# Last-window remainders as fp32 products in column groups, and side-by-side high and low tokens, in an attention + mixture-of-experts kernel

## The chip, the cores and the metric

One NeuronCore of a Trainium2 chip runs the whole kernel. The metric is device time in microseconds, the median of the runs. Names: PE is TensorE's matmul row, PEld its weight loads, DVE is VectorE, ACT is ScalarE, POOL is GpSimd, SP is SyncE, which issues the weight transfers.

## What is computed

Eight sequences of 576 tokens go through windowed attention (8 heads of 64, window 128, a distance bias), which gives 512 numbers per token, `x`. Each token then goes to one of eight experts:

```
e = argmax(logits[b, s])  if s == 0 or local_gate[b, s] < 0.5  else  the expert of token s-1
h = np.maximum(x[b, s] @ w1[e], 0.0)          # 512 -> 1024
out[b, s] = p[e] * (h @ w2[e])                # 1024 -> 512, p is the softmax gate
```

## The kernel before

The first third is attention, with an order of instructions written out by hand. It writes `x` to a DRAM table. After that the experts are run in **visits**: a list of (expert, number of rows) that is fixed when the program is built, in blocks of 32 rows. `PLAN` has three own visits (8, 12 and 12 blocks) and then twelve by rank: 16, 9, 12, 8, 12, 8, 12, 7, 14, 9, 6 and 5 blocks. Each is run by `Fixed.run`, one behind the other.

A visit with N = 32 x blocks rows has eight steps f (128 of the 1024 hidden units each). In step f, `h` (128 hidden x N rows, in PSUM) is the sum of four slices kc of three products each, and then `second(f-1)` adds the step before to the results `y`: one PSUM tile of 128 rows x 512 for each **window** of 128 rows, again three products per window and step. Three products stand for one, because each fp32 number is split into a high and a low float32r part (`cut` for weights, `xh`, `xl` in `qx` for tokens, `hh`, `hl` for hidden values): `three` (L1058) issues high x high, high x low and low x high at L1060, L1061 and L1062. `windows` (L51) gives the starts of the windows; the last one is moved back so that it is whole, and overlaps the one before it where the number of blocks is no multiple of 4 (9 blocks: starts 0, 4 and 5). Rows computed twice are dropped by the index table when results are scattered.

Between the two layers ACT makes `hh = relu(h)` (L1108) and DVE makes `hl = max(h, 0) - hh` (L1109). `second(f-1)` stands behind `h` of step f on PE, so this pair of instructions has the time of one `second` and one `h` to be done. At a visit's end `finish` scales each `y` by the gate, alternately on ACT (L1069) and DVE (L1067), and POOL scatters it (L1047).

Weights come in chunks of 512 KB, eight to a visit (`a` for the first layer, `b` for the second, alternating), 120 in all. `Stream.load` issues a transfer on SP's queue into one of six `wraw` buffers (L264); `Stream.split` makes the high part on ACT (L269, two casts per chunk) and the low part on DVE (L271, two subtractions), into one of six `cut` buffers. A chunk is split as soon as a `cut` buffer is free, so up to six are ready ahead. While visits run, `Feed` gathers the rows of later visits on POOL and turns them (`split_x`: DVE transpose L209, ACT cast L213, DVE subtraction L215). Engines take their instructions in program order, so each of these pieces also delays what stands behind it on its engine.

Of the kernel before, what the change touches and what calls it, by code (L numbers as in the profile page):

```python
# [10 lines left out]
F32 = mybir.dt.float32  # L11
F32R = mybir.dt.float32r
# [3 lines left out]
ALU = mybir.AluOpType  # L16
# [32 lines left out]


def windows(nb):  # L51
    return [min(4 * t, nb - 4) for t in range((nb + 3) // 4)]


PLAN = _plan()
# [45 lines left out]
def moe_attention(ctx, tc, qT, kT_d, vv, wg, wl, w1, w2, out):  # L101
# [32 lines left out]
    msel_last = cp.tile([P, 3, 4], F32, name="msel_last")  # L134
# [33 lines left out]
    def run(g):  # L168
        for _ in g:
            pass  # L170
# [103 lines left out]
    class Stream:  # L274


        def __init__(self, order):
            self.order = order
            self.raw, self.cut, self.gone, self.n_raw, self.n_cut, self.first, self.depth = [], {}, set(), 0, 0, 0, 1

        def load(self):
            while self.n_raw < len(self.order) and self.n_raw < self.n_cut + RAWS:
                e, which, c = self.order[self.n_raw]
                self.raw.append(load_chunk(e() if callable(e) else e, which, c))
                self.n_raw += 1

        def fill(self):
            while self.n_cut < len(self.order) and self.n_cut < self.first + self.depth:
                self.load()
                run(self.split(self.room(), now.act, nc.vector))  # L290
            self.load()

# [3 lines left out]

        def split(self, c, scalar, vector):
            raw = self.raw.pop(0)
            self.cut[self.n_cut] = c[:, 0], c[:, 1]
            self.n_cut += 1  # L300
            yield from split_chunk(raw, c, scalar, vector)
# [28 lines left out]
    FIXED_ORDER = [(w, c) for c in range(4) for w in "ab"]  # L330
    FLEX_ORDER = [(w, c) for w in "ab" for c in range(4)]
    order, by_rank = [], [expert_reg(r) for r in range(NE)]
    for kind, e, _, nb in PLAN:
        order += [(e if kind == "own" else by_rank[e], w, c) for w, c in (FLEX_ORDER if nb == 4 else FIXED_ORDER)]
    W = Stream(order)

    vp = ctx.enter_context(tc.tile_pool(name="vp", bufs=4))


    with ExitStack() as actx:  # L340
# [90 lines left out]
        def setup():  # L431

            whole = dict(channel_multiplier=0, allow_small_or_imprecise_dtypes=True)
            for a in (V[0][1][64:128], *zero_p(1), *zero_q(1), V[1][1][64:128], part[:, P + 64:]):
                pool.memset(a, 0.0)
                yield
            pool.memset(w32, 0.0)
            nc.sync.dma_start(w32[:, :, 0:8], wg.rearrange("(k p) e -> p k e", p=P))
            nc.sync.dma_start(w32[:, :, 8:9], wl.rearrange("(k p) e -> p k e", p=P))
            yield  # L440
            pool.memset(onesb, 1.0)
            yield
# [12 lines left out]
            pool.memset(first[0:1, 0:1], 1.0)  # L455
            yield
            pool.memset(msel_last, 0.0)
            yield
            for n in range(1, 4):
                pool.tensor_copy(msel_last[:, n - 1, 4 - n:], msel[:, 4 - n:])  # L460
# [322 lines left out]
        def indices(t, idx, x0, c0, visits):  # L783

            xi, rw, sc = idx
            wins = [(at + w, min(4, nb - 4 * i)) for at, nb in visits for i, w in enumerate(windows(nb))]
# [15 lines left out]
            while lo < n:  # L802
                hi = lo + 1
                at, new = wins[lo]
                while new == 4 and hi < n and wins[hi] == (wins[hi - 1][0] + 4, 4):
                    hi += 1
                sel = msel if new == 4 else msel_last[:, new - 1]
# [253 lines left out]
        nc.tensor.matmul(o, ah, bl, start=False, stop=False)  # L1061
        nc.tensor.matmul(o, al, bh, start=False, stop=stop)  # L1062

    def finish(o, g, col, alt):
        y = mp.tile([P, DM], F32, name="y", bufs=4)
        if alt:
            nc.vector.tensor_scalar(y, o, g, None, ALU.mult)  # L1067
        else:
            now.act.activation(y, o, AF.Copy, scale=g)  # L1069
        pending.append((col, y))  # L1070


    class Fixed:
        def __init__(self, rows):
            self.rows = rows

        def columns(self):
            return 96 * 32 * self.rows.blocks + 24 * DM * len(windows(self.rows.blocks))

        def run(self, W, tick):  # L1080
            N = 32 * self.rows.blocks
            wins = [slice(32 * w, 32 * w + P) for w in windows(self.rows.blocks)]
            n = len(wins)
            ys = [py.tile([P, DM], F32, name="y") for _ in range(n)]
            xh, xl = self.rows.xh[:, :, :N], self.rows.xl[:, :, :N]
            hs = {}

            def second(f):
                hh, hl = hs.pop(f)
                vh, vl = W.at("b")  # L1090
                for t, sl in enumerate(wins):
                    three(ys[t], hh[:, sl], hl[:, sl], vh[:, f % 2], vl[:, f % 2], f == 0, f == 7)
                    if t == n // 2 - 1:
                        tick()
                if f % 2:
                    W.done("b")

            for f in range(8):
                ah, al = W.at("a")
                hp = ph_.tile([P, N], F32, name="h")  # L1100
# [5 lines left out]
                hh = mp.tile([P, N], F32R, name="hh", bufs=3)  # L1106
                hl = mp.tile([P, N], F32R, name="hl", bufs=3)
                now.act.activation(hh, hp, AF.Relu)  # L1108
                nc.vector.scalar_tensor_tensor(hl, hp, 0.0, hh, ALU.max, ALU.subtract)  # L1109
                hs[f] = (hh, hl)  # L1110
                if f % 2:
                    W.done("a")
# [2 lines left out]
                    second(f - 1)  # L1115
                tick()
            second(7)
            for t in range(n):
                c = self.rows.t0 + t
                finish(ys[t], self.rows.g[:, t:t + 1], self.rows.idx[2][:, c:c + 1], t % 2)  # L1120


    class Flex:
# [238 lines left out]
```

## Time and profile before

| | us |
|---|---|
| median of 3 runs | 699.55 (698.94 to 699.76) |
| the profiled execution, its own time | 698.89 |
| its span in the profile | 697.2 |
| PE busy | 672.1 (96%) |
| DVE busy | 506.7 (73%) |
| ACT busy | 408.9 (59%) |
| POOL busy | 422.8 (61%) |

Busy time of PE is no measure of work done: products are pipelined, and each row's duration includes the time until its last results are out. The time that one product really costs is the step from its start to the start of the next.

### The profile page before, as it was taken

How to read it: one execution, taken by the hardware profiler on the slowest of the kernel's cores; microseconds unless marked ns; L12 is line 12 of the kernel's file. 1: busy time of each engine (PE TensorE's matmuls, PEld its weight loads, DVE VectorE, ACT ScalarE, POOL GpSimd, SP SyncE). 2: the span in 40 equal slices, each digit the busy share in tenths (PEclk: the TensorE clock that was granted, in tenths of full speed). 3: DMA queues.
4: the chain of work that ended last, by engine and by line, in shares of the span. 5: the costliest groups of instructions: out<-in, count | busy, mean ns of one | idle time of the engine just before them, and what ended most of it. 6: DMA issues, size and time to landing. Idle time of an engine off the chain costs nothing.

```text
span 697.2 us, 16242 instructions
## 1 busy us (share of the span) xinstructions
PE 672.1 (96%) x5377; PEld 563.1 (81%) x5377; DVE 506.7 (73%) x1738; ACT 408.9 (59%) x1157; POOL 422.8 (61%) x689
## 2 busy tenths in 40 slices
PE   8999999999889999999999999999999999999995
PEld 4777777777657778898888889899899888888994
DVE  7798988988887999996455985775675574455750
ACT  5987978979887753344334444554554563344540
POOL 8868678687896878077744554566467357151411
PEclk9999999999999999999999999999999999999998
DMA  8963753843643765364645555675675564355600
GB/s 269 316 210 121 236 178 122 263 152 115 198 153 101 234 228 181 117 200 156 176 139 170 166 173 152 216 228 165 195 224 176 187 212 161 122 177 162 210 31 20
DMA packets 65944, 122.23 MB, mean 175 GB/s; under 512 B 14177, under 2 KB 33249, under 8 KB 65858
## 3 DMA queue, kind: packets, MB, share of 16 engines
q1 hardware_dynamic: 56034, 101.27, 45.9%
q0 software_dynamic: 9392, 19.31, 9.2%
q8 instruction: 43, 0.70, 0.4%
q10 hardware_dynamic: 432, 0.59, 0.3%
q14 instruction: 43, 0.35, 0.1%
HBM read 102.14 MB, written 20.30 MB: 176 GB/s over the span
## 4 chain that ended last, share of the span: by engine, by line
PE 83%; DVE 6%; issue 4%; POOL 4%; ACT 2%; POOLq 0%; ACTq 0%; DVEq 0%
PE y L1062 10%; PE y L1060 10%; PE y L1061 10%; PE h L1061 10%; PE h L1062 10%; PE h L1060 10%; PE xa L188 7%; PE pt L188 6%; PE sc L188 6%; PE pk L188 3%; POOL ro_all L188 2%; DVE scs L188 1%; ACT cut L188 1%; POOL cut L188 1%; POOL out L1047 0%
## 5 line engine op out<-in xcount | busy, mean ns | idle before, releaser
L203 POOL DMA_INDIRECT kr<-xd,xidx x142 | 156.9, 1105 | 58.9 <-issue 42.7
L271 DVE TENSOR_TENSOR cut<-wraw,cut 128x512 fp32r<-128x512 f32 x232 | 151.1, 688 | 44.2 <-ACT cut L269 42.9
L269 ACT CAST cut<-wraw 128x512 fp32r<-128x512 f32 x218 | 124.3, 618 | 59.5 <-PE y L1062 57.8
L1061 PE MATMUL h<-qx,cut 128*128 128x384 f32 (+7 forms) x472 | 148.3, 314 | 0.2 <-DVE qx L215 0.2
L1062 PE MATMUL h<-qx,cut 128*128 128x384 f32 (+7 forms) x472 | 148.4, 314 | 0.0
L1060 PE MATMUL h<-qx,cut 128*128 128x384 f32 (+7 forms) x472 | 147.4, 313 | 0.0
L1047 POOL DMA_INDIRECT out<-y,sidx x41 | 44.7, 1089 | 145.2 <-ACT y L1069 117.6
L1062 PE MATMUL y<-cut,hl 128*128 128x512 f32 x328 | 129.6, 396 | 1.2 <-DVE hl L1109 1.1
L1060 PE MATMUL y<-cut,hh 128*128 128x512 f32 x328 | 130.0, 396 | 0.0
L1061 PE MATMUL y<-cut,hh 128*128 128x512 f32 x328 | 129.2, 394 | 0.0
L188 ACT ACTIVATE cut<-scs,mn 128x192 f32<-128x192 f32 (+1 forms) x288 | 124.8, 437 | 5.8 <-DVE mn L188 5.6
L188 POOL TENSOR_SCALAR cut<-cut,r 128x192 f32<-128x192 f32 (+1 forms) x288 | 116.1, 419 | 19.2 <-DVE r L188 9.9
L1108 ACT ACTIVATE hh<-h 128x384 fp32r<-128x384 f32 (+7 forms) x113 | 49.8, 441 | 124.1 <-PE h L1062 123.9
L1109 DVE SCALAR_TENSOR_TENSOR hl<-h,hh 128x384 fp32r<-128x384 f32 (+7 forms) x120 | 58.5, 488 | 77.0 <-ACT hh L1108 75.1
L1061 PEld LDWEIGHTS h<-qx,cut 128*128 128x128 f32 x472 | 89.2, 189 | 6.5 <-DVE qx L215 0.8
L1060 PEld LDWEIGHTS h<-qx,cut 128*128 128x128 f32 x472 | 89.3, 189 | 5.7
L1062 PEld LDWEIGHTS h<-qx,cut 128*128 128x128 f32 x472 | 89.2, 189 | 1.8
L188 PE MATMUL pt<-ident,cut 128*128 128x128 f32 x512 | 74.4, 282 | 2.4 <-POOL cut L188 2.3
L1062 PEld LDWEIGHTS y<-cut,hl 128*128 128x128 f32 x328 | 61.4, 188 | 16.6 <-DVE hl L1109 3.5
L188 DVE CUSTOM_DVE_ANT_0 scs<-sc,slopes 128x192 f32<-128x192 f32 (+1 forms) x224 | 67.4, 334 | 9.5 <-PE sc L188 6.3
L1060 PEld LDWEIGHTS y<-cut,hh 128*128 128x128 f32 x328 | 61.8, 188 | 9.7
L1061 PEld LDWEIGHTS y<-cut,hh 128*128 128x128 f32 x328 | 61.8, 188 | 9.6
(205 smaller groups left out, 976.8 us busy)
## 6 DMA issues: line engine op xcount, KB each, us to landing
wraw<-w SPq DMA_DIRECT2D x120, 512.0 KB
kr<-kT SPq DMA_DIRECT2D x31, 288.0 KB
qx<-qT SPq DMA_DIRECT2D x30, 288.0 KB
cut<-v SPq DMA_DIRECT2D x8, 1024.0 KB
xd<-T SPq DMA_DIRECT2D x8, 768.0 KB
xd<-T SPq DMA_DIRECT2D x8, 384.0 KB
kr<-xd,xidx POOLq DMA_INDIRECT x142, 3.9
qx<-qT SPq DMA_DIRECT2D x16, 64.0 KB
```

Of the source, the lines that this page charges most:

```text
L188: ins = getattr(self.engine, name)(*args, **kw)
L203: queued(nc.gpsimd.indirect_dma_start(out=r, out_offset=None, in_=src[0:n, :], in_offset=bass.IndirectOffsetOnAxis(ap=col, axis=0), bounds ...
L269: scalar.copy(c[:, 0, f], raw[:, f])
L271: vector.tensor_tensor(c[:, 1, f], raw[:, f], c[:, 0, f], ALU.subtract)
L1047: ins = nc.gpsimd.indirect_dma_start(out=out[:, :], out_offset=bass.IndirectOffsetOnAxis(ap=col, axis=0), in_=y, in_offset=None, bounds_ch ...
L1060: nc.tensor.matmul(o, ah, bh, start=start, stop=False)
L1061: nc.tensor.matmul(o, ah, bl, start=False, stop=False)
L1062: nc.tensor.matmul(o, al, bh, start=False, stop=stop)
L1108: now.act.activation(hh, hp, AF.Relu)
L1109: nc.vector.scalar_tensor_tensor(hl, hp, 0.0, hh, ALU.max, ALU.subtract)
```

## The change

1. `windows` no longer moves the last window back. Where the rest behind the whole windows is one or two blocks (32 or 64 rows; the visits of 9, 14, 9, 6 and 5 blocks), that rest has no float32r products any more. ACT takes relu of it into an fp32 tile `hr`, and `beside` multiplies `hr` with the raw fp32 weights `wraw`: four steps' products of 32 rows, or two steps' of 64 rows, stand in different column groups of TensorE and go to different partitions of one `y` tile. `finish` then adds the four (or two) partial sums on DVE, and takes this tile first. A rest of three blocks (the visit of 7) becomes a window of 96 rows.
2. The raw buffers of these visits' `b` chunks are kept until `beside` has read them.
3. In visits with fewer than 256 rows (7, 6 and 5 blocks) the first layer multiplies the high weights with high and low tokens side by side, in one product of 2N columns, and the low weights in one of N columns. ACT copies the half that belongs to the low tokens to SBUF (`ha`), DVE adds the other half, and DVE, not ACT, makes `hh`.

```diff
 def windows(nb):
-    return [min(4 * t, nb - 4) for t in range((nb + 3) // 4)]
+    return range(0, nb, 4)
...
         def load(self):
-            while self.n_raw < len(self.order) and self.n_raw < self.n_cut + RAWS:
+            while self.n_raw < len(self.order) and self.n_raw < min([self.n_cut, *self.kept]) + RAWS:
...
+            if self.n_cut in self.keep:
+                self.kept[self.n_cut] = raw
...
-    def finish(o, g, col, alt):
+    def finish(o, g, col, alt, groups=1):
         y = mp.tile([P, DM], F32, name="y", bufs=4)
+        m = o.shape[0] // groups
         if alt:
-            nc.vector.tensor_scalar(y, o, g, None, ALU.mult)
+            nc.vector.tensor_scalar(y[:m], o[:m], g[:m], None, ALU.mult)
         else:
-            now.act.activation(y, o, AF.Copy, scale=g)
-        pending.append((col, y))
+            now.act.activation(y[:m], o[:m], AF.Copy, scale=g[:m])
+        for j in range(1, groups):
+            nc.vector.scalar_tensor_tensor(y[:m], o[m * j:m * j + m], g[:m], y[:m], ALU.mult, ALU.add)
+        pending.append((col[:m], y[:m]))
...
+            def beside(f):
+                if f % 2:
+                    i = W.find("b")
+                    raws.append((i, W.kept[i]))
+                if f % groups < groups - 1:
+                    return
+                for j in range(groups):
+                    nc.tensor.matmul(ys[-1][m * j:m * j + m], rest[j], raws[j // 2][1][:, j % 2], start=f < groups, stop=f == 7,
+                                     skip_group_check=True)
...
             def second(f):
...
+                if m:
+                    beside(f)
+                for t in range(self.whole):
+                    sl = wins[t]
+                    three(ys[t][:sl.stop - sl.start], hh[:, sl], hl[:, sl], vh[:, f % 2], vl[:, f % 2], f == 0, f == 7)
...
-                    three(hp, ah[:, f % 2, cs], al[:, f % 2, cs], xh[:, kc], xl[:, kc], kc == 0, kc == 3)
+                    if both:
+                        passed[0] += 3 * N
+                        nc.tensor.matmul(hp.rearrange("p (two n) -> p two n", n=N), ah[:, f % 2, cs], self.rows.x[:, :, kc, :N],
+                                         start=kc == 0, stop=False, skip_group_check=True)
+                        nc.tensor.matmul(hp[:, :N], al[:, f % 2, cs], xh[:, kc], start=False, stop=kc == 3, skip_group_check=True)
+                    else:
+                        three(hp, ah[:, f % 2, cs], al[:, f % 2, cs], xh[:, kc], xl[:, kc], kc == 0, kc == 3)
...
-                now.act.activation(hh, hp, AF.Relu)
-                nc.vector.scalar_tensor_tensor(hl, hp, 0.0, hh, ALU.max, ALU.subtract)
+                if both:
+                    ha = mp.tile([P, N], F32, name="ha", bufs=2)
+                    now.act.copy(ha, hp[:, N:])
+                    nc.vector.tensor_tensor(ha, hp[:, :N], ha, ALU.add)
+                    hp = ha
+                w = P * self.whole if m else N
+                hh = mp.tile([P, N], F32R, name="hh", bufs=3)[:, :w]
+                hl = mp.tile([P, N], F32R, name="hl", bufs=3)[:, :w]
+                if m:
+                    rest.append(mp.tile([P, 64], F32, name="hr", bufs=8)[:, :m])
+                    now.act.activation(rest[-1], hp[:, w:], AF.Relu)
+                if both:
+                    nc.vector.tensor_scalar(hh, hp[:, :w], 0.0, None, ALU.max)
+                else:
+                    now.act.activation(hh, hp[:, :w], AF.Relu)
+                nc.vector.scalar_tensor_tensor(hl, hp[:, :w], 0.0, hh, ALU.max, ALU.subtract)
```

On PE, at the end of the last visit (5 blocks), before: `h` is a slice's first-layer product, `y` the second layer's; the six `y` products at the end are the last step's two windows.

```order
L1060 MATMUL h<-qx,cut 128x160
L1061 MATMUL h<-qx,cut 128x160
L1062 MATMUL h<-qx,cut 128x160
L1060 MATMUL y<-cut,hh 128x512
L1061 MATMUL y<-cut,hh 128x512
L1062 MATMUL y<-cut,hl 128x512
L1060 MATMUL y<-cut,hh 128x512
L1061 MATMUL y<-cut,hh 128x512
L1062 MATMUL y<-cut,hl 128x512
```

The same place after the change: two products per slice, and in front of the last step's only whole window the remainder's four fp32 products of steps 4 to 7.

```order
L1140 MATMUL h<-qx,cut 128x320
L1142 MATMUL h<-qx,cut 128x160
L1069 MATMUL y<-cut,hh 128x512
L1070 MATMUL y<-cut,hh 128x512
L1071 MATMUL y<-cut,hl 128x512
L1112 MATMUL y<-wraw,hr 32x512 x4
L1069 MATMUL y<-cut,hh 128x512
L1070 MATMUL y<-cut,hh 128x512
L1071 MATMUL y<-cut,hl 128x512
```

Six products of the second window are gone from each pair of steps, and the four side by side stand in front of the whole window's.

On DVE, from the end of the second visit of 9 blocks into the visit of 6, before:

```order
L1109 SCALAR_TENSOR_TENSOR hl<-h,hh 128x288
L271 TENSOR_TENSOR cut<-wraw,cut 128x512 x2
L1067 TENSOR_SCALAR y<-y,gs 128x512
L271 TENSOR_TENSOR cut<-wraw,cut 128x512 x2
L1109 SCALAR_TENSOR_TENSOR hl<-h,hh 128x192 x2
```

The same place after the change; `ha` is the sum of both halves of `h`:

```order
L1162 SCALAR_TENSOR_TENSOR hl<-h,hh 128x256
L271 TENSOR_TENSOR cut<-wraw,cut 128x512 x2
L1081 SCALAR_TENSOR_TENSOR y<-y,gs 32x512 x2
L271 TENSOR_TENSOR cut<-wraw,cut 128x512 x2
L1081 SCALAR_TENSOR_TENSOR y<-y,gs 32x512
L1150 TENSOR_TENSOR ha<-h,ha 128x192
L1159 TENSOR_SCALAR hh<-ha 128x128
L1162 SCALAR_TENSOR_TENSOR hl<-ha,hh 128x128
L1150 TENSOR_TENSOR ha<-h,ha 128x192
```

Three additions of partial sums take the place of one scaling, and each step of the short visit has three DVE instructions instead of one.

On ACT, in the visit of 6 blocks after the change:

```order
L1149 COPY ha<-h 128x192
L269 CAST cut<-wraw 128x512 x2
L1157 ACTIVATE hr<-ha 128x64
L1149 COPY ha<-h 128x192
L269 CAST cut<-wraw 128x512 x2
L1157 ACTIVATE hr<-ha 128x64
```

Before, one `hh<-h` stood in the place of the copy and of the relu; now the relu of the rest (`hr`, which PE's fp32 products read) waits for DVE's sum and stands behind two casts.

## Rows read from the trace of the kernel before

**Rows 1.** The page: busy time, and the slices of PE and its clock.
```profile
PE 672.1 (96%) x5377; PEld 563.1 (81%) x5377; DVE 506.7 (73%) x1738; ACT 408.9 (59%) x1157; POOL 422.8 (61%) x689
PE   8999999999889999999999999999999999999995
PEclk9999999999999999999999999999999999999998
```

**Rows 2.** Windows: the visits of 9, 7, 14, 9, 6, 5 blocks, in time.
```profile
core 0: us, PE busy (x) PEld busy (x) DVE busy (x) ACT busy (x) POOL busy (x), PEclk, DMA share, GB/s
374.60:406.00 31.40, 31.40 (x199) 27.16 (x198) 26.14 (x78) 13.87 (x28) 16.63 (x17) 1.00 0.56 177
552.30:574.70 22.40, 22.36 (x146) 19.69 (x145) 17.66 (x33) 14.21 (x30) 14.58 (x13) 1.00 0.68 223
574.70:616.10 41.40, 41.40 (x193) 36.03 (x192) 19.63 (x32) 15.90 (x30) 16.92 (x16) 1.00 0.47 147
616.10:645.40 29.30, 29.30 (x169) 26.17 (x168) 17.16 (x30) 13.91 (x28) 11.07 (x12) 1.00 0.56 170
645.40:667.20 21.80, 21.80 (x146) 19.78 (x146) 14.98 (x29) 12.94 (x28) 7.70 (x7) 1.00 0.55 174
667.20:689.20 22.00, 22.00 (x145) 19.51 (x143) 6.96 (x15) 6.53 (x16) 2.24 (x2) 1.00 0.04 16
```

**Rows 3.** Timeline of PE around 600 us: start, duration, instruction (14 blocks).
```profile
599.72 0.36 PE L1060 MATMUL h<-qx,cut 128*128 128x448 f32 x1
599.92 0.36 PE L1061 MATMUL h<-qx,cut 128*128 128x448 f32 x1
...
600.55 0.40 PE L1061 MATMUL y<-cut,hh 128*128 128x512 f32 x1
600.79 0.39 PE L1062 MATMUL y<-cut,hl 128*128 128x512 f32 x1
```

**Rows 4.** Timeline of PE: 7 blocks behind a `y` product; then 9 blocks.
```profile
570.33 0.40 PE L1062 MATMUL y<-cut,hl 128*128 128x512 f32 x1
570.56 0.26 PE L1060 MATMUL h<-qx,cut 128*128 128x224 f32 x1
570.66 0.28 PE L1061 MATMUL h<-qx,cut 128*128 128x224 f32 x1
570.77 0.27 PE L1062 MATMUL h<-qx,cut 128*128 128x224 f32 x1
...
639.83 0.29 PE L1061 MATMUL h<-qx,cut 128*128 128x288 f32 x1
639.96 0.29 PE L1062 MATMUL h<-qx,cut 128*128 128x288 f32 x1
```

**Rows 5.** Timeline of PE around 671 us, 5 blocks, behind a `y` product.
```profile
671.00 0.40 PE L1062 MATMUL y<-cut,hl 128*128 128x512 f32 x1
671.23 0.23 PE L1060 MATMUL h<-qx,cut 128*128 128x160 f32 x1
671.31 0.27 PE L1061 MATMUL h<-qx,cut 128*128 128x160 f32 x1
671.42 0.27 PE L1062 MATMUL h<-qx,cut 128*128 128x160 f32 x1
```

**Rows 6.** Timeline of PE around 123 us, fp32 products of attention.
```profile
122.58 1.19 PE L188 MATMUL pk<-xT,w 128*32 128x128 f32 x40
123.70 0.59 PE L188 MATMUL sc<-kr,qx 128*128 128x192 f32 x2
124.13 0.60 PE L188 MATMUL pt<-ident,cut 128*128 128x128 f32 x4
124.57 0.38 PE L188 MATMUL pk<-ident,part 128*128 128x128 f32 x2
```

**Rows 7.** Timeline of PE around 242 us: another tile form between float32r products.
```profile
242.16 0.28 PE L1062 MATMUL h<-qx,cut 128*128 128x256 f32 x1
242.28 0.28 PE L1060 MATMUL h<-qx,cut 128*128 128x256 f32 x1
242.49 0.38 PE L188 MATMUL pk<-identb,rcb 128*1 128x128 f16 x4
242.80 0.39 PE L1061 MATMUL h<-qx,cut 128*128 128x256 f32 x1
243.02 0.28 PE L1062 MATMUL h<-qx,cut 128*128 128x256 f32 x1
```

**Rows 8.** Groups of DVE by form: busy us, mean ns, idle before.
```profile
L271 DVE TENSOR_TENSOR cut<-wraw,cut 128x512 fp32r<-128x512 f32 x232 | 151.1, 688 | 44.2 <-ACT cut L269 42.9
L1109 DVE SCALAR_TENSOR_TENSOR hl<-h,hh 128x512 fp32r<-128x512 f32 x8 | 5.5, 691 | 13.0 <-ACT hh L1108 13.0
L1109 DVE SCALAR_TENSOR_TENSOR hl<-h,hh 128x192 fp32r<-128x192 f32 x8 | 2.8, 355 | 2.5 <-ACT hh L1108 2.5
L188 DVE TENSOR_TENSOR trk<-trk,tr 128x128 f32<-128x128 f32 x4 | 1.1, 271 | 0.0
L188 DVE TENSOR_SCALAR slopes<-qx 128x128 f32<-128x128 f32 x4 | 0.8, 249 | 0.3 <-POOL qx L188 0.3
```

**Rows 9.** Waits by engine and cause, 552 to 575 us.
```profile
DVE qx L215 <- ACT qx L213: 2.2, 4, 0.7
DVE cut L271 <- ACT cut L269: 2.0, 2, 1.2
```

**Rows 10.** Waits by engine and cause, 645 to 690 us: total, times, longest.
```profile
DVE qx L215 <- ACT qx L213: 1.1, 2, 0.7
```

**Rows 11.** The group of casts on ACT; below it SP's waits from 300 us on.
```profile
L269 ACT CAST cut<-wraw 128x512 fp32r<-128x512 f32 x218 | 124.3, 618 | 59.5 <-PE y L1062 57.8 <-DMA wraw<-w 1.5
SPq L264 <- DVE cut L271: 269.4, 82, 7.0
```

**Rows 12.** Timeline at the end of the last visit, all engines.
```profile
688.58 0.69 ACT L1069 ACTIVATE y<-y,gs 128x512 f32<-128x512 f32 x1 [1.83 <-PE y L1062]
...
688.84 0.40 PE L1062 MATMUL y<-cut,hl 128*128 128x512 f32 x1
689.28 0.75 DVE L1067 TENSOR_SCALAR y<-y,gs 128x512 f32<-128x512 f32 x1 [2.17 <-PE y L1062]
689.54 0.98 POOL L1047 DMA_INDIRECT out<-y,sidx  x1 [19.35 <-ACTq L1312]
690.83 0.99 POOL L1047 DMA_INDIRECT out<-y,sidx  x1 [0.30 <-issue]
```

More of the change, by code (lines that the diff above doesn't have):

```diff
@@ L133, in moe_attention @@
     quart = cp.tile([P, 4], F32, name="quart")
-    msel_last = cp.tile([P, 3, 4], F32, name="msel_last")
+    msel_part = cp.tile([P, 3, 4], F32, name="msel_part")
     roff = cp.tile([P, 1], F32, name="roff")
@@ L278, in __init__ @@
             self.order = order
+            self.keep, self.kept = set(), {}
             self.raw, self.cut, self.gone, self.n_raw, self.n_cut, self.first, self.depth = [], {}, set(), 0, 0, 0, 1
         def load(self):
-            while self.n_raw < len(self.order) and self.n_raw < self.n_cut + RAWS:
+            while self.n_raw < len(self.order) and self.n_raw < min([self.n_cut, *self.kept]) + RAWS:
                 e, which, c = self.order[self.n_raw]
@@ L289, in fill @@
                 self.load()
+                if not self.raw:
+                    break
                 run(self.split(self.room(), now.act, nc.vector))
@@ L332, in moe_attention @@
     order, by_rank = [], [expert_reg(r) for r in range(NE)]
+    kept = set()
     for kind, e, _, nb in PLAN:
+        if nb % 4 in (1, 2):
+            kept |= {len(order) + i for i, (w, _) in enumerate(FIXED_ORDER) if w == "b"}
         order += [(e if kind == "own" else by_rank[e], w, c) for w, c in (FLEX_ORDER if nb == 4 else FIXED_ORDER)]
     W = Stream(order)
+    W.keep = kept
     vp = ctx.enter_context(tc.tile_pool(name="vp", bufs=4))
@@ L456, in setup @@
             yield
-            pool.memset(msel_last, 0.0)
+            pool.memset(msel_part, 0.0)
             yield
             for n in range(1, 4):
-                pool.tensor_copy(msel_last[:, n - 1, 4 - n:], msel[:, 4 - n:])
+                pool.tensor_copy(msel_part[:, n - 1, :n], msel[:, :n])
                 yield
@@ L785, in indices @@
             xi, rw, sc = idx
-            wins = [(at + w, min(4, nb - 4 * i)) for at, nb in visits for i, w in enumerate(windows(nb))]
+            wins = [(at + w, min(4, nb - w)) for at, nb in visits for w in windows(nb)]
             m, n = t.shape[1], len(wins)
@@ L806, in indices @@
                     hi += 1
-                sel = msel if new == 4 else msel_last[:, new - 1]
+                sel = msel if new == 4 else msel_part[:, new - 1]
                 dve.tensor_tensor(fw[:, lo:hi], t[:, at:at + 4 * (hi - lo)].rearrange("p (c q) -> p c q", q=4),
@@ L1075, in __init__ @@
             self.rows = rows
+            self.n, part = rows.n, rows.last(rows.n - 1)
+            self.part = part if part < 3 else 0
+            self.whole = self.n - (self.part > 0)
         def columns(self):
-            return 96 * 32 * self.rows.blocks + 24 * DM * len(windows(self.rows.blocks))
+            return 96 * 32 * self.rows.blocks + (24 * self.whole + 8 * self.part) * DM
         def run(self, W, tick):
             N = 32 * self.rows.blocks
-            wins = [slice(32 * w, 32 * w + P) for w in windows(self.rows.blocks)]
-            n = len(wins)
-            ys = [py.tile([P, DM], F32, name="y") for _ in range(n)]
+            wins = [slice(P * t, min(P * t + P, N)) for t in range(self.n)]
+            ys = [py.tile([P, DM], F32, name="y") for _ in wins]
             xh, xl = self.rows.xh[:, :, :N], self.rows.xl[:, :, :N]
-            hs = {}
+            hs, rest, raws = {}, [], []
+            m = 32 * self.part
+            groups = P // m if m else 1
+            both = N < 256
+            def beside(f):
[7 more added lines that the diff above has]
+                                     skip_group_check=True)
+                passed[0] += 4 * DM
+                for i, _ in raws:
+                    del W.kept[i]
+                del rest[:groups]
+                raws.clear()
             def second(f):
@@ L1090, in second @@
                 vh, vl = W.at("b")
-                for t, sl in enumerate(wins):
-                    three(ys[t], hh[:, sl], hl[:, sl], vh[:, f % 2], vl[:, f % 2], f == 0, f == 7)
-                    if t == n // 2 - 1:
+                if m:
[3 more added lines that the diff above has]
+                    three(ys[t][:sl.stop - sl.start], hh[:, sl], hl[:, sl], vh[:, f % 2], vl[:, f % 2], f == 0, f == 7)
+                    if t == (self.n + 1) // 2 - 1:
                         tick()
@@ L1099, in run @@
                 ah, al = W.at("a")
[L1100 removed]
+                hp = ph_.tile([P, 2 * N if both else N], F32, name="h")
                 for kc in range(4):
                     cs = slice(P * kc, P * kc + P)
[L1103 removed]
+                    if both:
[5 more added lines that the diff above has]
+                        three(hp, ah[:, f % 2, cs], al[:, f % 2, cs], xh[:, kc], xl[:, kc], kc == 0, kc == 3)
                     if kc == 1:
                         tick()
[L1106 to L1109 removed]
+                if both:
[14 more added lines that the diff above has]
+                nc.vector.scalar_tensor_tensor(hl, hp[:, :w], 0.0, hh, ALU.max, ALU.subtract)
                 hs[f] = (hh, hl)
@@ L1117, in run @@
             second(7)
-            for t in range(n):
+            for i, t in enumerate([self.n - 1, *range(self.n - 1)] if m else range(self.n)):
                 c = self.rows.t0 + t
-                finish(ys[t], self.rows.g[:, t:t + 1], self.rows.idx[2][:, c:c + 1], t % 2)
+                rows = P if m and t == self.n - 1 else wins[t].stop - wins[t].start
+                finish(ys[t][:rows], self.rows.g[:, t:t + 1], self.rows.idx[2][:, c:c + 1], i % 2 and groups < 4, rows // (wins[t].stop - wins[t].start))
     class Flex:
```

## The prediction

> **What bounds the kernel now.** First the page: PE is busy for 96% of the span at the full clock, and DVE, the next, for 73% [rows 1]. That is an average, so I then cut out the visits that the change touches (the width of `h` in PE's timeline marks them). In each of the six PE is busy all the time, at a granted clock of 1.00 (2.4 GHz), while DVE's load differs: 17.66 of 22.40 us with 7 blocks, 14.98 of 21.80 with 6, 6.96 of 22.00 with 5 [rows 2]. So a product less on PE is time gained, but in the visits of 7 and 6 blocks DVE has only 5 and 7 us to spare.
>
> Third, what a product costs: the step from start to start. A `y` product of 512 columns takes 0.23 us, an `h` product of 448 columns 0.20 [rows 3], one of 288 columns 0.13 [rows 4]. Narrower ones gain nothing: with 224 and with 160 columns the step is 0.11, except just behind a `y` product, where it is 0.10 and 0.08 [rows 4, 5]. I read this as the weights' load showing: behind a long product the next weights are in place, behind a short one they are not.
>
> **The change, part by part.**
>
> *Removed.* Five visits (9, 14, 9, 6, 5 blocks) lose their last window: 8 steps of 3 products, 24 per visit, 120 in all. 120 x 0.23 = -27.6 us.
>
> *Added fp32 products.* No fp32 product of 512 columns is in the trace. The nearest are attention's: four fp32 instructions of 128 columns start at 124.13, the next group at 124.57, so 0.11 each [rows 6], about twice the float32r price per column. The tokens' logits are 20 products per sequence in the code (16 of 128 columns, 4 of 64) and 40 instructions in the row, so an fp32 product is two instructions. Those 40 stand in column groups of 32 (the row's 128*32). One behind another they would need 32 x 0.11 + 8 x 0.055 = 4.0 us; they took 1.12 (122.58 to 123.70) [rows 6]. So four groups do run side by side. At 512 columns an instruction is then 4 x 0.107 = 0.43 us, and a set of two or four products side by side 0.86. Rests of 32 rows (9, 9, 5 blocks) need two sets per visit, rests of 64 rows (14, 6) four: 6 + 8 = 14 sets, +12.0 us. One behind another, the 40 products would cost 34.4; that is the upper end, and 12.0 the lower.
>
> *Changing the form.* Each set stands between float32r products of the whole array. A small tile form between such products costs 0.09 on entry (242.28 to 242.49, where 0.12 is usual), about 0.08 on the way back (four products of 128 columns, 0.23, take 0.31) and 0.10 at the step after (0.22 instead of 0.12) [rows 7]: 0.27 per set, +3.8 us. With 512 columns behind it the last 0.10 may be hidden: lower end 2.4.
> The Trainium skill (TensorEngine Tiling (Array Packing), section Key Properties) says that changing the tiling mode drains TensorE. Taken at its word, each of 28 changes would wait out the tail of a product, 0.40 - 0.23 = 0.17 us [rows 3], which makes 4.8 us in place of 3.8, and the forecast 1 us later; the row's 0.09 and 0.08 say less than a whole drain. I keep 3.8.
>
> *Side by side.* 7, 6 and 5 blocks have 32 slices each, now three steps of 0.11 (0.33). After: one product of 448, 384 or 320 columns and one of 224, 192 or 160. The long ones cost 0.20, 0.174 and 0.145 (the latter two on the line from 0.13 at 288 to 0.20 at 448). Each short one stands behind a long one, as in the two places where the step was 0.10 and 0.08; for 192 columns I take 0.09. Gains per slice: 0.03, 0.07 and 0.11; times 32: 1.0, 2.2 and 3.6, -6.8 us. If the short product cost its 0.11 here too, it would be -4.7.
>
> PE's own work: -27.6 + 12.0 + 3.8 - 6.8 = **-18.6 us**.
>
> *DVE in the short visits.* Each step gets a sum (`ha`) and a max (`hh`), and with 6 and 5 blocks a narrower `hl`. Neither is in the trace. Nearest: a sum of an SBUF and a PSUM tile of 128 columns, 0.271; a tensor-scalar of 128 columns, 0.249; the slope over columns from `hl`, (0.691 - 0.355) / 320 = 1.05 ns [rows 8]. So per step 0.37 + 0.35 with 224 columns; 0.34 + 0.25 - 0.07 with 192; 0.31 + 0.25 - 0.03 with 160. Over eight steps: +5.8, +4.2 and +4.2.
>  - 7 blocks: 17.66 + 5.8 = 23.5 us of DVE against 22.4 - 1.0 = 21.4 of PE. It no longer fits: a stall of 2.1, if the 4.2 us in which DVE now waits for ACT's casts [rows 9] fill up.
>  - 6 blocks: 14.98 + 4.2 + three additions for the 9 blocks' rest at about 0.69 (an `hl` of 512 columns has that length [rows 8]) - 0.3 for the scaling they replace = 20.9; 1.1 in which DVE waits for ACT's token casts [rows 10] does not go away: 22.0. PE needs 21.8 - 5.5 + 4 x 1.13 - 2.2 = 18.6. Stall 3.4.
>  - 5 blocks: 11.2 of DVE in 15.1 of PE, but at the start the sum for step 0 stands behind a scaling and an addition of the visit before (0.75, 0.69) and two subtractions (1.3): ready after 3.3 us, while PE has two `h`, 8 x 0.22 = 1.8. Stall 1.5. And `hr` waits on ACT for DVE's sum, behind casts of 0.62 [rows 11]: 0.4 at each of two sets. Together 2.3.
>
> In all +7.8 us. Its lower end is 0 (chunks are split up to six ahead, which would have to absorb it), its upper end twice this, if ACT and DVE wait for each other at each step.
>
> *The end.* Now ACT scales the first `y` while PE still runs, DVE the second; scatters start at 689.54 and 690.83 [rows 12]. After, the rest's tile needs ACT (0.69) and three dependent additions (3 x 0.69) once its last set is done, 0.8 us before PE's end. So it is ready 2.0 us after PE instead of 0.3, and the other scatter queues behind it on POOL: +2.0.
> In other visits the additions are covered by two `h` of the visit that follows (3 us or more with 8 or more blocks).
>
> *Raw buffers kept longer.* Loads wait for a buffer now (269 us on SP's queue), and yet casts waited only 1.5 us in the whole run for a load [rows 11]. Priced 0, covered by the chunks split ahead; without that cover late loads of the last two visits could cost some 3 to 5 us. *A rest of 96 rows* (7 blocks): same number of products, 0. *Index tables*: a few small DVE instructions, 0.
>
> **Sum.** -18.6 + 7.8 + 2.0 = -8.8 us. The profiled execution took 698.89, 0.66 under the median, so 690.1 for it and **690.8 for the median**.
>
> **Rivals.**
>  - *DVE's additions are hidden.* For it: DVE has idle time in all three visits, and chunks are ready ahead. Against: program order puts subtractions between the new instructions. Then -18.6 + 2.0: 683.0.
>  - *DVE and ACT take it all back.* Stalls of 15.6 in place of 7.8: -1.0, 698.5, no change. For it: sum, relu of the rest and casts form a chain ACT, DVE, ACT in program order. Against: with 14, 9 and 9 blocks nothing of this arises, and they alone bring 1.0 + 2 x 3.2 us.
> The Trainium skill (TensorEngine Tiling (Array Packing), section PSUM Bottleneck) warns of a neighbour of this: that packing speeds up TensorE but not the reading of PSUM, which can become the bound. Here that would be the additions in `finish`.
>  - *Late weights.* The kept buffers hold loads back where PE got faster: 3 to 5 us more, 695.
>  - *The column groups don't overlap* (the other side): every product waits for the one before it, because each has its own `hr` and raw chunk to wait for. 40 products then cost 34.4 instead of 12.0: 690.8 + 22.4 = 713. It decides from about 40% of the overlap lost (8.8 of 22.4). Against: the tokens' row, whose products read different token tiles too.
>
> **Chances.** Forecast (687 to 694) 0.53; hidden 0.17; taken back 0.12; late weights 0.12; no overlap 0.06. The range leaves out the last and half of the taken-back case at the top, and the far part of the hidden case at the bottom: 683 to 697.5. A change under 0.2% (1.4 us) can hardly be told from none here; faster by more than that has 0.88, within it 0.06, slower 0.06.
>
> **What would show it.** Right: fp32 `y` rows start within a few ns of each other, and the next set some 0.86 us on; `h` pairs in the last visit 0.22 apart; the first visit of 9 blocks some 3 us shorter, that of 14 some 1 us; the visits of 7 and 6 not shorter, with DVE nearly always busy; the last scatter 2 us farther from PE's end. Wrong: fp32 products 0.43 apart, gaps of PE in front of `L1112`, casts waiting for loads, or PE without gaps in the short visits.

## The result and the profile after

Four runs gave a median of **692.52 us** (690.85 to 693.42) against 699.34 us (698.94 to 699.76) before: a ratio of 0.990, 95% interval 0.988 to 0.992, 6.8 us less. The forecast was 690.8, range 683.0 to 697.5.

The page of the profiled execution, span and busy time, to be read beside [rows 1]:

```profile
span 689.2 us, 16062 instructions
PE 657.8 (95%) x5241; PEld 536.2 (78%) x5241; DVE 520.8 (76%) x1794; ACT 414.7 (60%) x1200; POOL 424.6 (62%) x689
```

PE has 136 instructions and 14 us of busy time less, DVE 14 us more. The windows of the same six visits, in time (9, 7, 14, 9, 6, 5 blocks), answer to [rows 2] and have its columns:

```profile
373.91:402.05 28.14, 28.14 (x191) 23.03 (x190) 25.11 (x72) 15.46 (x38) 15.76 (x15) 1.00 0.55 176
548.34:573.36 25.02, 22.83 (x113) 17.55 (x112) 22.16 (x49) 13.86 (x30) 15.27 (x13) 1.00 0.52 172
573.36:614.35 40.99, 40.99 (x185) 32.02 (x184) 19.69 (x33) 16.54 (x38) 14.79 (x15) 1.00 0.42 125
614.35:640.47 26.12, 26.12 (x161) 21.93 (x160) 16.82 (x31) 14.57 (x37) 13.98 (x13) 1.00 0.55 178
640.47:662.70 22.23, 21.00 (x105) 14.69 (x104) 19.53 (x47) 14.45 (x37) 6.36 (x6) 1.00 0.76 236
662.70:681.07 18.37, 16.96 (x105) 13.07 (x103) 11.87 (x33) 7.86 (x24) 2.29 (x2) 1.00 0.15 48
```

Lengths of the visits, before [rows 2] and after, beside what the terms of the prediction give for each:

| visit | before | after | change | predicted |
|---|---|---|---|---|
| 9 blocks, first | 31.4 | 28.1 | -3.3 | -3.2 |
| 7 blocks | 22.4 | 25.0 | **+2.6** | +1.1 |
| 14 blocks | 41.4 | 41.0 | -0.4 | -1.0 |
| 9 blocks, second | 29.3 | 26.1 | -3.2 | -3.2 |
| 6 blocks | 21.8 | 22.2 | +0.4 | +0.2 |
| 5 blocks | 22.0 | 18.4 | -3.6 | -4.5 |

The two visits of 9 blocks are 6.4 us shorter together and the last one 3.6; the other three are 2.6 us longer together. In the short visits (7, 6 and 5 blocks) PE, which was hardly idle there before (0.04 us), now waits: 2.2, 1.2 and 1.4 us of them are not busy. PE's timeline at the start of the visits of 7 and of 6 blocks shows where:

```profile
550.74 0.26 PE L1142 MATMUL h<-qx,cut 128*128 128x224 f32 x1
552.17 0.50 PE L1069 MATMUL y<-cut,hh 128*128 128x512 f32 x1 [1.17 <-DVE hh L1159]
...
644.11 0.50 PE L1069 MATMUL y<-cut,hh 128*128 128x512 f32 x1 [1.23 <-DVE hh L1159]
```

Two steps of `h` are done, and the first `y` waits for step 0's `hh`. ACT and DVE at the same place tell why it is late:

```profile
549.59 0.68 ACT L1079 ACTIVATE y<-y,gs 128x512 f32<-128x512 f32 x1
550.17 0.61 ACT L213 CAST qx<-xtr 128x512 fp32r<-128x512 f32 x1
550.67 0.35 ACT L1149 COPY ha<-h 128x224 f32<-128x224 f32 x1
...
550.81 0.69 DVE L215 TENSOR_TENSOR qx<-xtr,qx 128x512 fp32r<-128x512 f32 x1 [0.32 <-ACT qx L213]
551.42 0.38 DVE L1150 TENSOR_TENSOR ha<-h,ha 128x224 f32<-128x224 f32 x1
```

The copy of the low half stands on ACT behind the scaling that ends the visit before and a cast of tokens for a later visit; the sum stands on DVE behind the other half of that token work, which itself waited for ACT. What was one relu on ACT is now a copy, a sum and a max, with a queue in front of each engine. With 7 blocks this wait is 1.2 of the 2.2 us. Of the rest, 0.6 come one step later, in front of the `y` of 555.68: there the copy of step 1 stands on ACT behind a cast of tokens that waits 2.2 us for DVE's transpose.

### The profile page after: what moved, and what is told of

Its sections match the earlier page's. It is cut to its first block, busy times and chain, and to the rows that moved or that the text cites. A ratio compares the mean times of both kernels' runs of the same rounds, so it can differ in the third digit from the quotient of the medians.

```text
span 689.2 us, 16062 instructions
## 1 busy us (share of the span) xinstructions
PE 657.8 (95%) x5241; PEld 536.2 (78%) x5241; DVE 520.8 (76%) x1794; ACT 414.7 (60%) x1200; POOL 424.6 (62%) x689
## 5 line engine op out<-in xcount | busy, mean ns | idle before, releaser
L203 POOL DMA_INDIRECT kr<-xd,xidx x142 | 159.7, 1125 | 58.9 <-issue 42.7
L188 POOL TENSOR_SCALAR cut<-cut,r 128x192 f32<-128x192 f32 (+1 forms) x288 | 115.7, 416 | 19.5 <-DVE r L188 10.3
L1070 PE MATMUL h<-qx,cut 128*128 128x384 f32 (+4 forms) x376 | 122.0, 324 | 0.2 <-DVE qx L215 0.2
L1071 PE MATMUL h<-qx,cut 128*128 128x384 f32 (+4 forms) x376 | 122.1, 325 | 0.0
L1069 PE MATMUL h<-qx,cut 128*128 128x384 f32 (+4 forms) x376 | 122.0, 325 | 0.0
L1069 PE MATMUL y<-cut,hh 128*128 128x512 f32 (+1 forms) x288 | 115.6, 402 | 4.5 <-DVE hh L1159 4.4
L1071 PE MATMUL y<-cut,hl 128*128 128x512 f32 (+1 forms) x288 | 113.9, 397 | 1.6 <-DVE hl L1162 1.5
L1070 PE MATMUL y<-cut,hh 128*128 128x512 f32 (+1 forms) x288 | 113.6, 394 | 0.0
L1162 DVE SCALAR_TENSOR_TENSOR hl<-h,hh 128x384 fp32r<-128x384 f32 (+2 forms) x96 | 48.9, 510 | 61.6 <-ACT hh L1161 60.3
L1161 ACT ACTIVATE hh<-h 128x384 fp32r<-128x384 f32 (+2 forms) x89 | 40.9, 459 | 80.0 <-PE h L1071 79.8
L1070 PEld LDWEIGHTS h<-qx,cut 128*128 128x128 f32 x376 | 70.8, 188 | 5.4 <-DVE qx L215 0.8
L1069 PEld LDWEIGHTS h<-qx,cut 128*128 128x128 f32 x376 | 70.9, 188 | 4.7
L1069 PEld LDWEIGHTS y<-cut,hh 128*128 128x128 f32 (+1 forms) x288 | 53.9, 187 | 25.4 <-DVE hh L1159 6.7
L1071 PEld LDWEIGHTS h<-qx,cut 128*128 128x128 f32 x376 | 70.8, 188 | 1.8
L188 PE MATMUL sc<-kr,qx 64*64 64x192 f32 (+2 forms) x1088 | 64.9, 320 | 3.9 <-issue 1.8
L188 PE MATMUL xa<-pts,cut 128*64 128x128 f32 (+2 forms) x640 | 67.9, 336 | 0.4 <-ACT xT L188 0.4
```

Of the source, the lines that this page charges most:

```text
L188: ins = getattr(self.engine, name)(*args, **kw)
L203: queued(nc.gpsimd.indirect_dma_start(out=r, out_offset=None, in_=src[0:n, :], in_offset=bass.IndirectOffsetOnAxis(ap=col, axis=0), bounds ...
L1069: nc.tensor.matmul(o, ah, bh, start=start, stop=False)
L1161: now.act.activation(hh, hp[:, :w], AF.Relu)
L1162: nc.vector.scalar_tensor_tensor(hl, hp[:, :w], 0.0, hh, ALU.max, ALU.subtract)
```

## The experiments

Medians are of this many runs, each with the ratio to the kernel before on the same chip.

**The change once more.** No edit.

> The changed kernel once more, as the measure for the others. The change's median over four runs was 692.5, its profiled run 690.9. If what takes time back were a steady stall, five more rounds give 692 to 693 and a second profile shows the same gaps of PE: 1.4 us at the start of the visits of 7, 6 and 5 blocks. If the profiled run was a lucky one, the second profile has longer gaps there, by the 1.7 us in which the two differ.

692.79 us (692.35 to 694.06, 5 runs), ratio 0.9912 (0.9899 to 0.9926). Its trace has the same visits (22.20 us with 6 blocks) and the same waits. It is 1.5 us longer than the first, from parts that the change does not touch: the first expert product starts at 226.80 instead of 225.50, and the two visits of 12 blocks take 71.25 instead of 70.88 us. So the first profiled run, the fastest of nine, flatters the change by 1 to 2 us; the medians are the measure.

**No pairs.** The fp32 remainders stay.

```
-            both = N < 256
+            both = False
```

> The fp32 remainders stay, high and low tokens again take three products each in the visits of 7, 6 and 5 blocks. Theory (the stalls belong to the pairs: sum, max and the copy on ACT): the pairs save 4.7 us of products in the steps and cost 7.8 us of stalls, so without them 3.1 us less than the changed kernel, about 689.4; the visit of 7 blocks back at 22.4 us, 6 blocks at 21.3, 5 blocks at 18.8. Rival (the stalls of 6 and 5 blocks belong to the remainder's additions and its relu): only the 7 blocks gain their 2.6, the other two lose the 4.0 that the pairs save there, 1.4 us more than the changed kernel, about 694.

689.72 us (689.40 to 691.17, 4 runs), ratio 0.9872 (0.9857 to 0.9887): 3.1 us less than the change, as the theory had it. Windows of the visits of 7, 6 and 5 blocks:

```profile
549.73:572.08 22.35, 22.31 (x146) 19.02 (x145) 17.57 (x33) 14.17 (x30) 14.57 (x13) 1.00 0.59 191
639.10:660.43 21.33, 21.32 (x138) 16.08 (x136) 15.70 (x31) 13.83 (x37) 6.13 (x6) 1.00 0.76 246
660.43:679.31 18.88, 18.88 (x137) 15.27 (x135) 7.59 (x17) 6.94 (x24) 2.28 (x2) 1.00 0.15 47
```

PE is busy without a break. So the remainder's additions and its relu, without pairs, leave PE no idle time.

**Pairs alone.** The kernel before, with this in its visits below 256 columns (and the sum and max of the change behind it):

```
+                        nc.tensor.matmul(hp.rearrange("p (two n) -> p two n", n=N), ah[:, f % 2, cs], self.rows.x[:, :, kc, :N], ...)
+                        nc.tensor.matmul(hp[:, :N], al[:, f % 2, cs], xh[:, kc], start=False, stop=kc == 3, skip_group_check=True)
```

> The kernel before with the side-by-side products alone, windows as before, no fp32 products. Theory (the stalls belong to the pairs): 7 blocks 2.6 us longer than before, 6 blocks -1.6 of products and some 2 of stall, 5 blocks -2.4 and 1.5 of stall; in all 1 to 3 us slower than before, 700.5 to 702.5. Rival (in 6 and 5 blocks the stalls come from the remainder): 7 blocks +2.6, 6 blocks -1.6, 5 blocks -2.4, so 1.4 us faster than before, 698.

700.94 us (698.64 to 702.18, 8 runs), ratio 1.0019 (1.0007 to 1.0032): slower, at the low end of the theory's span. The three visits:

```profile
553.66:578.68 25.02, 22.84 (x113) 18.17 (x112) 22.15 (x49) 13.86 (x30) 15.27 (x13) 1.00 0.62 199
649.36:671.15 21.79, 21.20 (x113) 17.82 (x112) 18.91 (x45) 12.45 (x28) 7.55 (x7) 1.00 0.54 174
671.15:691.59 20.44, 19.82 (x113) 17.15 (x111) 11.33 (x31) 6.44 (x16) 2.12 (x2) 1.00 0.04 17
```

7 blocks take the same 25.0 us as in the change, 6 blocks what they took before, 5 blocks 1.6 less. Against [rows 2] only the 5 blocks gain from the pairs. The three visits together are some 1 us longer. In this trace the first expert product also starts 1.4 us later than before (227.93 against 226.57), which no edit touches: it lies anywhere between 225.5 and 227.9 in the traces from chips like this one, and the two traces of the change have it 1.3 us apart.

**Two steps ahead.** In visits with pairs, `h` runs two steps ahead of `y`.

```
-                if f > 0:
-                    second(f - 1)
+                ahead = 2 if both else 1
+                if f >= ahead:
+                    second(f - ahead)
                 tick()
+            if ahead == 2:
+                second(6)
             second(7)
```

> The changed kernel with one edit: in the visits with pairs TensorE runs two steps of h ahead of y instead of one. Theory (the stall is latency: the chain copy, sum, max, slope of step 0 is late when two h are done): a third h of 1.0 to 1.3 us covers most of the 1.4 at the start of each of the three visits, 2.5 to 3.5 us less than the changed kernel, about 689.5. Rival (the stall is VectorE's throughput, busy for 22.2 of 25.0 us with 7 blocks): the wait only moves to later steps, less than 1 us gained, about 692.

**688.14 us** (686.34 to 688.59, 5 runs), ratio 0.9832 (0.9819 to 0.9846): 4.7 us less than the change, more than the 2.5 to 3.5 of the theory, and the fastest kernel measured. It does the same work on every engine, so throughput was not what held the visits up. Windows of 7, 6 and 5 blocks, and PE where the first `y` used to wait:

```profile
549.99:572.94 22.95, 21.92 (x113) 17.57 (x112) 21.09 (x48) 13.84 (x30) 15.41 (x13) 1.00 0.59 186
640.05:660.70 20.65, 19.69 (x105) 14.40 (x104) 19.08 (x47) 14.11 (x37) 6.10 (x6) 1.00 0.78 242
660.70:678.32 17.62, 16.60 (x105) 12.94 (x103) 11.60 (x34) 7.62 (x24) 2.17 (x2) 1.00 0.19 65
```
```profile
552.39 0.26 PE L1142 MATMUL h<-qx,cut 128*128 128x224 f32 x1
553.51 0.47 PE L1140 MATMUL h<-qx,cut 128*128 128x448 f32 x1 [0.86 <-DVE ha L1150]
...
554.87 0.40 PE L1069 MATMUL y<-cut,hh 128*128 128x512 f32 x1
```

The first `y` no longer waits; now the third `h` does, for one of two PSUM buffers, which the sum (`ha`) sets free. That is what is left: about 1 us per visit. With 7 blocks DVE is now busy for 21.1 of 22.95 us, so there its throughput may come next.
Less idle time of PE is only 1.8 of the 4.4 us that the three visits lose. Another 1.5 come from the last set of fp32 products of the visits of 6 and 5 blocks, which waits in the change for the rest's relu (`hr`) of the last step, and here no longer: 1.1 and 0.4 us (the rows of the first stand below, under the stalls). The last 1.1 are not traced. So the extra step helps at a visit's end as well as at its start.

**The relu of the sum on ScalarE.** The change with `hh` by ACT in all visits.

```
-                if both:
-                    nc.vector.tensor_scalar(hh, hp[:, :w], 0.0, None, ALU.max)
-                else:
-                    now.act.activation(hh, hp[:, :w], AF.Relu)
+                now.act.activation(hh, hp[:, :w], AF.Relu)
```

> The changed kernel with hh's relu back on ScalarE in the visits with pairs, for the same reason once more. Theory (latency of the chain at each visit's start): 0 to 2 us more than the changed kernel, 692.5 to 694.5. Rival (VectorE's throughput in the visit of 7 blocks): 1 to 2 us less there, about 691.

693.41 us (693.00 to 693.95, 4 runs), ratio 0.9926 (0.9909 to 0.9942), which can't be told from the change's 0.9912. The visits of 7 and 14 blocks (taken together, as three `h` products of the second stand among the last `y` of the first here) take 65.90 us, 66.01 and 65.91 in the two traces of the change, though DVE was relieved of eight max operations of 0.28 us. That agrees with the theory, but does not decide by itself: the edit also puts a change of engine into the chain, which could cost what the relief brings.

**One column group.** All products of a remainder accumulate in one group, without additions.

```
-                    nc.tensor.matmul(ys[-1][m * j:m * j + m], rest[j], ..., start=f < groups, stop=f == 7,
+                    nc.tensor.matmul(ys[-1][:m], rest[j], ..., start=f < groups and j == 0, stop=f == 7 and j == groups - 1,
```

> The changed kernel with all products of a remainder in one column group, accumulated there in PSUM, so that no additions are left in finish. If the column groups really run side by side: a set of four 32-column products takes 4 x 0.87 us instead of 0.87, one of two 64-column products 2 x 0.95, so 6 x 3 x 0.87 + 8 x 0.95 = 23 us more of products, less 1 to 3 us of additions and tail, 712 to 716. If the starts 6 to 7 ns apart only show when products were queued and they ran one behind another: no more than 1 us of difference. The row of a lone 32-column product also tells whether 0.474 us in sets of 64 rows against 0.434 in sets of 32 comes from the width of the group.

This and five more runs came to two chips on which the kernel before itself took 792 us (781 to 806), so their times say little: here 821.25, ratio 1.038 (1.030 to 1.047). The products can be read all the same. PE's timeline with one group, sets of 32 and of 64 rows:

```profile
762.50 3.62 PE L1112 MATMUL y<-wraw,hr 128*32 128x512 f32 x8
766.05 0.50 PE L1069 MATMUL y<-cut,hh 128*128 128x512 f32 x1
...
706.64 1.93 PE L1112 MATMUL y<-wraw,hr 128*64 128x512 f32 x4
708.50 0.50 PE L1069 MATMUL y<-cut,hh 128*128 128x512 f32 x1
```

And in the change, with a group each, what stands before and behind the set shown too:

```profile
671.06 0.34 PE L1140 MATMUL h<-qx,cut 128*128 128x320 f32 x1
671.24 0.24 PE L1142 MATMUL h<-qx,cut 128*128 128x160 f32 x1
671.31 0.35 PE L1140 MATMUL h<-qx,cut 128*128 128x320 f32 x1
671.50 0.23 PE L1142 MATMUL h<-qx,cut 128*128 128x160 f32 x1
671.67 1.06 PE L1112 MATMUL y<-wraw,hr 128*32 128x512 f32 x8
672.66 0.50 PE L1069 MATMUL y<-cut,hh 128*128 128x512 f32 x1
673.00 0.39 PE L1070 MATMUL y<-cut,hh 128*128 128x512 f32 x1
...
582.92 1.08 PE L1112 MATMUL y<-wraw,hr 128*64 128x512 f32 x4
583.92 0.50 PE L1069 MATMUL y<-cut,hh 128*128 128x512 f32 x1
```

From the set's start to the next product it is 3.55 us one behind another and 0.99 side by side for four products, 1.86 and 1.00 for two. The groups do overlap, at 3.6 and 1.9 times. By these rows the rival's price is 6 x 2.56 + 8 x 0.86 = 22 us, as the prediction had it.
The Trainium skill (TensorE: Matmul & The Clock Gate, section Why this matters for your kernels) gives 2.38 times for three groups of 32 rows; no run here has three, and these rows fall on either side.

**Pairs only with 6 and 5 blocks, two ahead**, and the same **with late additions**:

```
-            both = N < 256
+            both = N < 224
...
+                if f == both:
+                    while late:
+                        late.pop(0)()
+                    ys.extend(py.tile([P, DM], F32, name="y") for _ in wins)
```

> Two steps of h ahead of y, and pairs only in the visits of 6 and 5 blocks. By the traces of the two parts: the visit of 7 blocks takes 22.35 us as without pairs, against 22.95 with pairs two steps ahead, so 0.6 us less than that kernel, about 687.5. Rival (VectorE's relief in the visit of 7 blocks is given back, as chunks split ahead there were a stock for the visits that follow): no difference, 688.1 or more.

> The kernel with pairs for 6 and 5 blocks two steps ahead, and the remainder's additions of a visit issued behind the first two steps of the next. Theory (what is left of the stall at the start of 6 blocks, 1.2 us, is the first sum, which stands behind three additions on VectorE and holds back the PSUM buffer for the third h): the first sum comes two additions (1.5 us) earlier, that wait of 1.2 us goes, about 0.5 to 1.2 us less than without the edit, 686.3 to 687. Rival (the wait moves to the first y, since two additions now stand between sum, max and slope): no difference.

Both went to a chip of 792 us, a second try of each to the other, and a first try of the relu on ScalarE had been there too (798.41 us, ratio 1.010, 1.003 to 1.018). There the first expert visit alone took 57.55 us, where the change took 33.98 on another chip; windows of the one and of the other:

```profile
228.43:285.98 57.55, 35.70 (x263) 27.84 (x262) 32.90 (x104) 21.03 (x49) 23.59 (x26) 0.82 0.45 140
...
226.80:260.78 33.98, 32.00 (x262) 25.95 (x261) 32.68 (x104) 21.04 (x49) 27.52 (x26) 1.00 0.74 235
```

PE idled for 22 us, and the data came at 140 instead of 235 GB/s. Why was not found. The ratios there, 1.001 and 1.007 without and 0.992 and 0.991 with late additions, contain whatever keeps PE idle on these chips, and so don't answer the question asked. A third try of the second kernel had a chip like the first:

> Both edits on the kernel two steps ahead: no pairs with 7 blocks, and the remainder's additions behind the first two steps of the next visit; a third time, in the hope of a chip on which weights arrive in time. Theory: 7 blocks 22.35 us instead of 22.95; 6 blocks about 1 us less than the 20.65 of the kernel two steps ahead; 686 to 687.5 in all. Rivals: the visits that follow the 7 blocks or the first y of the 6 blocks give it back, 688.

690.39 us (689.14 to 690.64, 4 runs), ratio 0.9876 (0.9859 to 0.9892): slower than two steps ahead by itself. One half came out: 7 blocks take 22.34 us. The other turned over: 6 blocks take 22.27 us instead of 20.65. ACT, DVE and PE at the start of that visit:

```profile
641.39 1.25 ACT L1079 ACTIVATE y<-y,gs 128x512 f32<-128x512 f32 x2
642.55 0.29 ACT L1151 COPY ha<-h 128x192 f32<-128x192 f32 x1
642.68 0.74 DVE L1081 SCALAR_TENSOR_TENSOR y<-y,gs 32x512 f32<-32x512 f32 x1 [0.38 <-ACT y L1079]
643.45 0.36 DVE L1152 TENSOR_TENSOR ha<-h,ha 128x192 f32<-128x192 f32 x1
643.86 0.44 PE L1142 MATMUL h<-qx,cut 128*128 128x384 f32 x1 [1.30 <-DVE ha L1152]
```

The scalings now stand two in a row on ACT ahead of the copy `ha`, and an addition still stands ahead of the sum. Written later in the program, the rest's work was not put behind the chain on the engines. This start costs 0.3 us more than two steps ahead (a wait of 1.30 instead of 0.96), and the last set of the visit 0.5 (1.53 us to the next product instead of 1.01); the other 0.8 are short delays in between. The short visits make 1.1 of the 2.0 us between the two traces; the first expert product starts 1.4 us later. Whether pairs for 6 and 5 blocks alone would reach the 687.5 that the parts give was not measured on an undisturbed chip.

## Why the prediction came out

**Removed, -27.6.** 120 products at 0.227 to 0.231 us: holds.

**Sets and their form changes, +12.0 and +3.8.** The overlap is shown above. A set takes 0.99 to 1.00 us to the next product. It comes 0.10 late (671.50 to 671.67, where 0.07 is usual), and the step behind it is 0.34 instead of 0.23 (672.66 to 673.00). Together some 1.2 us, x 14 = 16.8 in place of 15.8. Two visits of 9 blocks agree: 24 x 0.231 - 2 x 1.2 = 3.1, measured 3.2 to 3.3. The 14 blocks would give 0.7 and gave 0.4.
With the drain of the Trainium skill (TensorEngine Tiling (Array Packing), section Key Properties) the two terms would be 16.8. That is what was measured in all, so the rows no longer speak against that rule; whether a drain is what they show stays open.

**Side by side, -6.8.** This term was too large (0.11 x 32 is 3.5 and not 3.6, too, which makes 6.7). Pairs start 0.25 to 0.26 us apart (671.06 to 671.31) and not 0.22. The short product's step is 0.07 (671.24 to 671.31), but the long one behind it then takes 0.18 to 0.19 instead of the 0.145 of its columns; I read this as the weights that a short product leaves no time to load, one step later. The rows of [rows 4, 5], from which the short step was taken, stood behind a `y` and ahead of a product whose own step was already the full 0.11. Per step of four pairs, `h` now takes 1.25, 1.12 and 1.00 us (without a set behind it) against 1.33, 1.32 and 1.30: 0.7, 1.6 and 2.4 us per visit, 4.7 in all. That was the lower bound.

**Stalls of the short visits, +7.8.** The sum holds: what the other terms leave of the changes of the visits is 3.3, 2.8 and 1.9 us, 8.0, where 2.1, 3.4 and 2.3 were forecast. For 5 blocks the mechanism holds too: the first `y` waits 1.4 us, and one of the two sets for `hr`:

```profile
679.13 0.14 PEld L1112 LDWEIGHTS y<-wraw,hr 128*32 128x32 f32 x2 [0.25 <-ACT hr L1157]
```

That set takes 1.37 us to the next product instead of 0.99; the other waits for nothing. The reason given for the 7 and 6 blocks does not hold. There the stall was counted as VectorE's load, 23.5 us in 21.4 and 22.0 in 18.6; DVE was busy for 22.2 of 25.0 and 19.5 of 22.2 us, and running one step further ahead with the same load took 2.1 and 1.6 us off the visits. The cause is the length of the chain from `h` to `hh` and `hr`, with only one step of `h` to cover it. That the sum came out all the same is luck.
In the visit of 6 blocks this shows at the end as well, which the prediction did not see, though it had the same wait for 5 blocks: the last set is split by a `y` product, and the two products that should overlap run apart. PE's timeline, and the row of ACT for `hr` of the last step:

```profile
659.70 1.07 PE L1112 MATMUL y<-wraw,hr 128*64 128x512 f32 x2
660.70 0.49 PE L1069 MATMUL y<-cut,hh 128*128 128x512 f32 x1
661.12 1.07 PE L1112 MATMUL y<-wraw,hr 128*64 128x512 f32 x2
662.13 0.50 PE L1070 MATMUL y<-cut,hh 128*128 128x512 f32 x1
...
660.41 0.26 ACT L1157 ACTIVATE hr<-ha 128x64 f32<-128x64 f32 x1
```

From 659.70 to 662.13 it is 2.4 us, where an unsplit set and one `y` take 1.3: 1.1 of the 2.8. The split itself costs little: the second product needs this `hr`, ready at 660.67, so an unsplit set would have waited for it and ended about as late (an estimate from these rows: 660.67 + 1.01 + 0.34 = 662.02). Without pairs and with two steps ahead the set is whole and waits for nothing.

**The end, +2.0.** Measured +0.2, 1.8 too much. The last rows of DVE and POOL:

```profile
680.92 2.31 DVE L1081 SCALAR_TENSOR_TENSOR y<-y,gs 32x512 f32<-32x512 f32 x3 [1.52 <-ACT y L1079]
682.06 0.99 POOL L1056 DMA_INDIRECT out<-y,sidx  x1 [15.54 <-ACTq L1366]
683.51 0.88 POOL L1056 DMA_INDIRECT out<-y,sidx  x1 [0.46 <-DVEq L1366]
```

The additions end 2.2 us behind PE, as forecast, but the scatter of the whole tile does not queue behind that of the rest; it goes first, at 682.06. The last scatter starts 2.4 us behind PE's end instead of 1.6 [rows 12], and the span ends 5.6 us behind that start instead of 6.3. It now carries 32 rows, not 128; in the eight traces from chips like the first the stretch is 6.3 to 6.4 us with 128 rows and 5.6 to 6.0 with 32.

**Rivals.** Hidden additions: half true, since without pairs they cost PE nothing; but the pairs' own instructions were not hidden. Taken back: the pairs as a whole are taken back, and more (3.1 us), the remainders are not. Late weights: no gap of PE in these windows ends with a load. No overlap: shown wrong. Of the signs, `h` pairs 0.22 apart (0.25) and the last scatter 2 us farther from PE's end (0.9) did not come; DVE was busy for 89 and 88% of the visits of 7 and 6 blocks, short of nearly always.

The sum by what was measured: -27.5 + 16.8 - 4.7 + 8.0 + 0.2 = -7.2 us against a forecast of -8.8, and 6.4 to 6.8 by the medians. Side by side 2.1 less and sets 1.0 more, against 1.8 at the end, leave 1.3 of the 1.6 us between the two sums. So part of the closeness is luck: terms off by 2.1, 1.8 and 1.0 us stand against each other. The two profiled executions are 8.0 us apart, more than this sum, since the first expert product starts 1.1 us earlier in the second (225.50 against 226.57), where the change does nothing.

## What to carry to other kernels

An edit of two parts is priced in two parts: here the remainders alone bring 9.5 us, the pairs lose 1.7 by themselves and 3.1 on top of the remainders, and together they still looked like a gain. A chain that gets longer is not priced by an engine's busy time but by the steps that the waiting engine can run ahead; count the queue in front of each link at the places where the run-ahead is shortest, which here are the start and the end of a visit, and try one step more of it before taking work off the engine.

## What had not been expected of the hardware

An fp32 product of 512 columns takes 2 x 0.43 us behind another of its form, but the first instruction of a set took 0.45 us with 32 columns of weights and 0.48 with 64 (in the trace with one group), and a set of two 64-column products costs as much time as one of four 32-column ones (1.00 and 0.99 us).
An addition of 32 rows takes as long as a scaling of 128, the nearest in these traces: 0.742 and 0.751 us, by the groups of DVE in the last visit and in that of 7 blocks (0.69 had been forecast for it):

```profile
L1081 DVE SCALAR_TENSOR_TENSOR y<-y,gs 32x512 f32<-32x512 f32 x1 | 0.7, 742 | 1.5 <-ACT y L1079 1.5
...
L1077 DVE TENSOR_SCALAR y<-y,gs 128x512 f32<-128x512 f32 x1 | 0.8, 751 | 1.1 <-PE y L1071 1.1
```

And there is a wait at a place that no edit touches. DVE around 328 us after the change:

```profile
327.45 0.71 DVE L209 STREAM_TRANSPOSE xtr<-kr 128x512 f32<-128x512 f32 x1 [1.50 <-DMA kr<-xd,xidx]
```

DVE waits for a gather of tokens, and `hl`, queued behind it (328.09), holds up a `y` product. The step of PE there was 0.44 us in this trace, 0.82 in the second of the same kernel and 1.15 two steps ahead, where 0.23 is usual. All five traces with both parts of the change from chips like the first have such a step (0.41 and 0.51 in the other two); the kernels before, without pairs and with pairs alone have none. Why was not found.
